# Windowed attention and a sticky mixture of experts on one core: the 128-partition attention transfers cut into 120 and 8 partitions

## The chip, the core and the metric

The kernel runs on one core of a Trainium2 chip, as one launch. The metric is the device time of the launch in microseconds (us). The core has five engines that run their own instruction streams: TensorE (PE in the profile, its weight loads PEld), VectorE (DVE), ScalarE (ACT), GpSimd (POOL) and SyncE (SP). Bulk data moves by DMA transfers, which an engine only issues; here SP issues all loads, ACT issues the stores of attention's result, and POOL issues the indirect gathers and scatters of the expert part.

## The reference

Two stages. The first is attention for 8 batches and 8 heads, with 32 global rows and 512 local rows of 64 numbers: a global row sees every row, a local row sees the global rows and the local rows at most 32 away. The second stage sends every token (a row of 8 x 64 = 512 numbers) through one of eight experts; a token keeps the expert of the token before it unless a local gate says otherwise.

```python
s_ll = np.where(np.abs(pos[:, None] - pos[None, :]) <= 32, s_ll, -1000000000.0)
out_l = softmax(concat([s_lg, s_ll])) @ concat([v_g, v_l])
...
fresh_e = argmax(x @ w_gate)
e = fresh_e if s == 0 or sigmoid(x @ w_local) < 0.5 else prev_e
out[b, s] = softmax(x @ w_gate)[e] * (relu(x @ w1[e]) @ w2[e])
```

## The kernel before

**Attention** runs from the start to about 275 us. Two heads make a pair, four pairs a batch, 32 pairs in all, numbered 0 to 31 here. A pair needs two loads of 128 partitions: its queries and keys (`load`, 128 x 1056 floats, 528 KB, array `qk`), and its values (`loadv`, 128 x 2080 floats, 1040 KB, array `vw`). A batch needs one more (`load_g`, 128 KB, its global queries). Query-and-key tiles stand in a ring of eight buffers (`hhl_a`, `wp_a`, `xhl_a`, `xr_a`, `raw` 0 to 3), value tiles in a ring of seven (`v` 0 to 3, `hhl_a`, `wp_a`, `v` 4; the names `hhl_a` and `wp_a` hold tiles of both kinds in different columns). `run` issues the loads ahead: queries and keys five pairs, values four pairs before the pair at which it stands. A load waits until the last reader of its buffer is done.

For each pair POOL copies the keys into `kx` (`prep`, L194), PE makes the scores (L240), DVE takes maximum and difference (L245, L247), ACT the exponential (L251), PE transposes (L257), ACT copies the result from PSUM into `pt` (L259), and PE multiplies with the values (L271). Work on the global rows (L291, L309, L323, L334) stands between pairs.

**The row stores.** When a batch is done and its keys and probabilities for the experts are made, `f4` writes its rows to the DRAM array `xs`, from which the experts gather. It issues six transfers on ACT: one of 128 partitions with four rows of 528 floats in each (1056 KB, L407), four of 32 partitions for the global rows (`xg`, 16 KB each, L411), and one of 2 KB (`gx`, L412). ACT runs its stream in order, so that the copies and exponentials behind these six wait until the last is issued. There are eight such stores, one for each batch; the first six fall among the pairs, the last two beside the first experts.

**Semaphores of transfers.** SP's and ACT's transfers share eight completion semaphores, DMAHW0 to DMAHW7, which are given out in turn when the program is built. A transfer first waits for the transfer that last held its semaphore, so at most eight are under way, and a store on ACT can wait for a load on SP, or the other way round. The turns go by the order in which the builder expects the transfers to be issued.

**Experts** fill the rest. Expert weights are loaded by SP into tiles of 512 KB (L1147), split by ACT and DVE into two parts (L1157, L1167), and used in PE's long runs of L1259 and L1270. The first three expert blocks overlap with the end of attention.

Of the kernel before, what the change touches and what calls it, by code (L numbers as in the profile page):

```python
# [18 lines left out]
P = 128  # L19
# [37 lines left out]
STORE = 2  # L57
AHEAD = 5
AHEADV = 4


def col(b):
    return 4 * b if b < NA else 4 * b + 1


def gcol(hf):
    return 4 * NA if hf == 0 else NT - 1
# [33 lines left out]
class Attn:  # L101
# [64 lines left out]
    def setup(self):  # L166
# [5 lines left out]
        yield  # L172
        nc.sync.dma_start(self.xs[0:P], zr)

    def load(self, b, pr):
        nc = self.nc
        if pr == 0:
            self.cur[b] = {"v": []}
        c = self.cur[b]
        t = c[("qk", pr)] = self.ld()  # L180
        nc.sync.dma_start(t, self.qk[b, pr])

    def load_g(self, b):
        g = self.cur[b]["qg"] = self.qgb()
        self.nc.sync.dma_start(g, self.qg[b])

    def loadv(self, b, pr):
        nc = self.nc
        v = self.v()
        self.cur[b]["v"].append(v)  # L190
        nc.sync.dma_start(v.rearrange("p w c -> p (w c)"), self.vw[b, pr])

    def cp(self, out, in_, pat):
        self.nc.gpsimd.affine_select(out=out, in_=in_, pattern=pat, compare_op=ALU.is_ge, fill=0.0, base=0, channel_multiplier=0)  # L194
# [205 lines left out]
    def f4(self, b, rt):  # L400
        nc = self.nc
        c = self.cur.pop(b)
        xa, xg = c["xa"], c["xg"]
        hf, b4 = b // 4, b % 4
        rq = slice(32 * b4, 32 * b4 + 32)
        r0 = P * (1 + col(b))
        nc.scalar.dma_start(self.xs[r0:r0 + 4 * P].rearrange("(t p) r -> p t r", p=P), xa)  # L407
        r0 = P * (1 + gcol(hf)) + 32 * b4
        xsg = self.xs[r0:r0 + 32]
        for h in range(4):  # L410
            nc.scalar.dma_start(xsg[:, 0:DM].rearrange("q (a h d) -> q a h d", a=2, h=4)[:, :, h], xg[32 * h:32 * h + 32])  # L411
        nc.scalar.dma_start(xsg[:, DM:ROW], rt.gx[rq])  # L412

    def run(self, rt, moe):
# [20 lines left out]
        for k in range(1, AHEAD):  # L435
            b, i = pairs[k]["u"]
            self.load(b, i)
            if i == 0 or k == 1:
                self.load_g(b)
            if k <= AHEADV:  # L440
                self.loadv(*pairs[k - 1]["u"])
# [11 lines left out]
        for s in range(n):  # L453
# [8 lines left out]
            if nl:  # L462
                if npr + AHEAD < len(pairs):
                    b, i = pairs[npr + AHEAD]["u"]
                    self.load(b, i)
                    if i == 0:
                        self.load_g(b)
                if npr + AHEADV < len(pairs):
                    self.loadv(*pairs[npr + AHEADV]["u"])
                npr += 1  # L470
# [1109 lines left out]
```

## Time and profile before

| what | value |
|---|---|
| median of three runs | 729.78 us (729.25, 729.78 and 739.17) |
| the profiled execution | 738.59 us, span 736.9 us |
| mean granted TensorE clock in it | 0.959 |
| PE busy | 661.8 us, 90% of the span |
| DVE, ACT, POOL busy | 422.4, 343.9 and 152.5 us |
| bytes by SP's queue (q1) | 117.72 MB |
| bytes by ACT's queue (q10) | 9.33 MB |
| attention's transfers of 128 partitions | 72 loads (32 + 32 + 8) and 8 row stores |

The profiled execution stands near the upper of the three runs, 8.8 us above their median. In the profile, "ACTq" and "SPq" are the issue of transfers on these engines: such a row's duration is the time in which the engine could do nothing else, not the time of the transfer, which is shown apart as the time to landing. Times in rows of the timeline and of the chain are counted from the start of the span.

### The profile page before, as it was taken

How to read it: one execution, taken by the hardware profiler on the slowest of the kernel's cores; microseconds unless marked ns; L12 is line 12 of the kernel's file. 1: busy time of each engine (PE TensorE's matmuls, PEld its weight loads, DVE VectorE, ACT ScalarE, POOL GpSimd, SP SyncE). 2: the span in 40 equal slices, each digit the busy share in tenths (PEclk: the TensorE clock that was granted, in tenths of full speed). 3: DMA queues.
4: the chain of work that ended last, by engine and by line, in shares of the span. 5: the costliest groups of instructions: out<-in, count | busy, mean ns of one | idle time of the engine just before them, and what ended most of it. 6: DMA issues, size and time to landing. Idle time of an engine off the chain costs nothing.

```text
span 736.9 us, 20404 instructions
## 1 busy us (share of the span) xinstructions
PE 661.8 (90%) x8277; PEld 551.8 (75%) x8277; DVE 422.4 (57%) x1052; ACT 343.9 (47%) x613; POOL 152.5 (21%) x259
## 2 busy tenths in 40 slices
PE   8689888687878869989899899999999999999996
PEld 6467656565656558779688788988888988988994
DVE  6566666655678666689732663533553634436563
ACT  4355545453545446464432753524353525345463
POOL 6112111121102130203121430304031202031122
PEclk9889989989989998999999999999999999999999
DMA  9976575847561455777662765725564725435763
GB/s 355 412 302 261 194 298 200 303 176 259 189 210 61 152 177 182 273 224 240 196 244 84 239 216 193 230 94 174 180 201 141 239 75 169 139 138 184 270 235 116
DMA packets 43019, 151.57 MB, mean 206 GB/s; under 512 B 7965, under 2 KB 9245, under 8 KB 38688
## 3 DMA queue, kind: packets, MB, share of 16 engines
q1 hardware_dynamic: 28368, 117.72, 45.5%
q0 software_dynamic: 6960, 21.90, 9.2%
q10 hardware_dynamic: 7456, 9.33, 3.7%
q8 instruction: 85, 1.39, 0.8%
q14 instruction: 150, 1.23, 0.5%
HBM read 130.55 MB, written 19.69 MB: 204 GB/s over the span
## 4 chain that ended last, share of the span: by engine, by line
PE 77%; DVE 10%; issue 5%; ACTq 3%; ACT 2%; DMA 1%; POOL 0%; DVEq 0%; POOLq 0%
PE ps L1270 27%; PE ps L1259 24%; PE ps L240 5%; PE ps L271 4%; PE ps L257 4%; PE ps L1212 3%; PE ps L347 2%; ACTq L411 2%; PE ps L291 2%; PE ps L334 2%; PE ps L323 2%; DMA xs<-xg 1%; DVE wp L1167 1%; DVE pe L247 1%; DVE mx L245 1%
## 5 line engine op out<-in xcount | busy, mean ns | idle before, releaser
L1270 PE MATMUL ps<-wp,wq 128*128 128x512 f32 x504 | 128.0, 401 | 1.0 <-ACT wq L1373 1.0
L1259 PE MATMUL ps<-wp,wp 128*128 128x256 f32 (+6 forms) x672 | 107.8, 320 | 1.5 <-issue 1.5
L1270 PEld LDWEIGHTS ps<-wp,wq 128*128 128x128 f32 x504 | 93.5, 190 | 20.8 <-ACT wq L1373 1.2
L1259 PEld LDWEIGHTS ps<-wp,wp 128*128 128x128 f32 x672 | 103.4, 189 | 5.5 <-issue 2.0
L1276 POOL DMA_INDIRECT out_dram<-y,tk x39 | 40.5, 1040 | 321.2 <-ACT y L1275 248.0
L1262 DVE SCALAR_TENSOR_TENSOR wq<-ps,wq 128x256 fp32r<-128x256 f32 (+6 forms) x80 | 41.3, 519 | 72.9 <-ACT wq L1261 65.2
L1261 ACT ACTIVATE wq<-ps 128x256 fp32r<-128x256 f32 (+6 forms) x80 | 36.8, 463 | 78.5 <-PE ps L1259 69.8
L1215 DVE TENSOR_TENSOR wp<-ps,wp 128x512 fp32r<-128x512 f32 x40 | 27.5, 691 | 79.7 <-ACT wp L1214 79.7
L245 DVE TENSOR_REDUCE mx<-ps 128x4 f32<-128x512 f32 x64 | 43.9, 685 | 36.4 <-PE ps L240 36.1
L1275 ACT ACTIVATE y<-ps,pp 128x512 f32<-128x512 f32 x39 | 26.9, 689 | 77.2 <-PE ps L1270 71.1
L251 ACT ACTIVATE pe<-pe 128x512 f32<-128x512 f32 x64 | 40.5, 633 | 40.8 <-DVE pe L247 40.3
L1167 DVE TENSOR_TENSOR wp<-raw,wp 128x1024 fp32r<-128x1024 f32 x47 | 56.9, 1217 | 2.8 <-ACT wp L1157 2.8
L1198 POOL DMA_INDIRECT xa<-xs,idx x42 | 51.3, 1221 | 17.1 <-issue 9.7
L259 ACT COPY pt<-ps 128x512 f32<-128x512 f32 x64 | 35.1, 595 | 40.3 <-DMA xs<-xg 17.7
L1157 ACT CAST wp<-raw 128x1024 fp32r<-128x1024 f32 x49 | 50.8, 1047 | 5.2 <-issue 3.8
L1214 ACT CAST wp<-ps 128x512 fp32r<-128x512 f32 x40 | 23.4, 590 | 55.2 <-PE ps L1212 55.2
L271 PE MATMUL ps<-v,pt 128*32 128x65 f32 x1536 | 31.4, 231 | 15.5 <-ACT pt L259 7.2
L247 DVE TENSOR_TENSOR pe<-ps,mx 128x512 f32<-128x512 f32 x64 | 44.1, 688 | 1.4
L1270 PE MATMUL ps<-hhl,wq 128*128 128x512 f32 x174 | 44.8, 398 | 0.0
L271 PEld LDWEIGHTS ps<-v,pt 128*32 128x32 f32 x1536 | 25.8, 115 | 25.1 <-ACT pt L259 10.4
L194 POOL TENSOR_SCALAR_AFFINE_SELECT kx<-raw 128x128 f32<-128x128 f32 (+1 forms) x64 | 21.9, 366 | 102.4 <-issue 76.9
L257 PE MATMUL ps<-idf,pe 128*128 128x128 f32 x256 | 39.9, 305 | 1.4 <-ACT pe L251 1.4
(284 smaller groups left out, 1168.5 us busy)
## 6 DMA issues: line engine op xcount, KB each, us to landing
raw<-in_w_dram SPq DMA_DIRECT2D x78, 512.0 KB, 4.1
v<-in_vw_dram SPq DMA_DIRECT2D x24, 1040.0 KB, 9.3
xa<-in_w_dram SPq DMA_DIRECT2D x26, 512.0 KB, 3.9
xT<-in_w_dram SPq DMA_DIRECT2D x20, 512.0 KB, 3.7
raw<-in_qk_dram SPq DMA_DIRECT2D x16, 528.0 KB, 6.5
xs<-xa ACTq DMA_DIRECT2D x8, 1056.0 KB, 7.4
hhl_a<-in_vw_dram SPq DMA_DIRECT2D x4, 1040.0 KB, 11.2
wp_a<-in_vw_dram SPq DMA_DIRECT2D x4, 1040.0 KB, 4.8
```

The lines of the kernel that those rows point to most:

```text
L245: nc.vector.tensor_reduce(out=mx, in_=st["sp"][h], axis=AX.X, op=ALU.max)
L247: nc.vector.tensor_tensor(out=st["pe"][:, 4 * h:4 * h + 4], in0=st["sp"][h], in1=mx.broadcast_to([P, 4, P]), op=ALU.subtract)
L251: self.nc.scalar.activation(out=pe, in_=pe, func=AF.Exp, scale=SCALE)
L257: nc.tensor.transpose(tp[:, i], st["pe"][:, 4 * hb + i], self.cst.idf)
L271: nc.tensor.matmul(o[32 * w4:32 * w4 + 32, t], pt[:, t, w4, :], v[:, 4 * t + w4, h * (D + 1):(h + 1) * (D + 1)], start=True, stop=True, sk ...
L1157: nc.scalar.copy(out=hi, in_=raw)
L1167: (nc.gpsimd if pool else nc.vector).tensor_tensor(out=lo, in0=raw, in1=hi.bitcast(F32), op=ALU.subtract)
L1198: self.nc.gpsimd.indirect_dma_start(out=self.xr[j] if k == "early" else self.xr4[:, j], out_offset=None, in_=src, in_offset=bass.IndirectO ...
L1259: nc.tensor.matmul(ph, a[:, dc, fs], b_[:, dc, n0:n1], start=(n == 0), stop=(n == 11))
L1262: nc.vector.scalar_tensor_tensor(out=hl[:, fc, n0:n1], in0=ph, scalar=0.0, in1=hh[:, fc, n0:n1].bitcast(F32), op0=ALU.max, op1=ALU.subtract)
L1270: nc.tensor.matmul(py, a[:, fc, js], b_[:, fs], start=(fc == 0 and k == 0), stop=(fc == 7 and k == 2))
L1276: sc = nc.gpsimd.indirect_dma_start(out=self.out, out_offset=bass.IndirectOffsetOnAxis(ap=self.g[1][:, j:j + 1], axis=0), in_=y, in_offset ...
```

## The change

Each of attention's loads of 128 partitions, and each row store, is made by two transfers, one of partitions 0 to 119 and one of partitions 120 to 127, on the same engine and one right after the other. The loads of weights, the small stores and the indirect transfers stay as they are, and so does all arithmetic.

```diff
+CUT = 120
...
+    def get(self, to, of):
+        for r in (slice(0, CUT), slice(CUT, P)):
+            self.nc.sync.dma_start(to[r], of[r])
...
-        nc.sync.dma_start(t, self.qk[b, pr])
+        self.get(t, self.qk[b, pr])
...
-        self.nc.sync.dma_start(g, self.qg[b])
+        self.get(g.rearrange("p a h q -> p (a h q)"), self.qg[b])
...
-        nc.sync.dma_start(v.rearrange("p w c -> p (w c)"), self.vw[b, pr])
+        self.get(v.rearrange("p w c -> p (w c)"), self.vw[b, pr])
...
-        nc.scalar.dma_start(self.xs[r0:r0 + 4 * P].rearrange("(t p) r -> p t r", p=P), xa)
+        x = self.xs[r0:r0 + 4 * P].rearrange("(t p) r -> p t r", p=P)
+        for r in (slice(0, CUT), slice(CUT, P)):
+            nc.scalar.dma_start(x[r], xa[r])
```

SP issues 72 transfers more and ACT eight more. They take turns at the same eight semaphores, so these turn over about twice as fast. Three places show it.

The first is ACT's stream at the row store of batch 0, before and after; the row behind the transfers is the copy into `pt` of the pair under way (`xa0` is the batch's rows, `xg0` its global rows, a number behind a name is that of the buffer).

```order
L407 DMA xs_57<-xa0_104 128x4x528 [waits DMAHW7_49]
L411 DMA xs_57<-xg0_107 32x2x64 [waits DMAHW0_49]
L411 DMA xs_57<-xg0_107 32x2x64 [waits DMAHW1_49]
L411 DMA xs_57<-xg0_107 32x2x64 [waits DMAHW2_49]
L411 DMA xs_57<-xg0_107 32x2x64 [waits DMAHW3_49]
L412 DMA xs_57<-gx_287 32x16 [waits DMAHW4_49]
L259 COPY pt2_140<-ps4_67 128x512 [waits PE_49,Activation_49]
```

```order
L412 DMA xs_57<-xa0_104 120x4x528 [waits DMAHW2_49]
L412 DMA xs_57<-xa0_104 8x4x528 [waits DMAHW4_49]
L416 DMA xs_57<-xg0_107 32x2x64 [waits DMAHW6_49]
L416 DMA xs_57<-xg0_107 32x2x64 [waits DMAHW0_49]
L416 DMA xs_57<-xg0_107 32x2x64 [waits DMAHW1_49]
L416 DMA xs_57<-xg0_107 32x2x64 [waits DMAHW2_49]
L417 DMA xs_57<-gx_300 32x16 [waits DMAHW4_49]
L262 COPY pt2_140<-ps4_67 128x512 [waits PE_49,Activation_49]
```

Before, the six transfers hold six different semaphores. After, the turns of SP's loads lie between them, and the last `xg` transfer waits for DMAHW2, which the 120-partition store took five rows above it, while the `gx` transfer waits for DMAHW4, which the 8-partition store took.

The second is SP's stream around the same store, before and after: the loads from the values of pair 10 (`v2`) to those of pair 12 (`hhl_a`).

```order
L191 DMA v2_132<-in_vw_dram 128x2080 [waits DMAHW2_49,PE_49]
L181 DMA xr_a_86<-in_qk_dram 128x1056 [waits DMAHW3_49,Pool_49]
L191 DMA v3_133<-in_vw_dram 128x2080 [waits DMAHW4_49,PE_49]
L181 DMA raw0_77<-in_qk_dram 128x1056 [waits DMAHW5_49,PE_49,Pool_49]
L185 DMA qgb1_149<-in_qg_dram 128x256 [waits DMAHW6_49,PE_49]
L191 DMA hhl_a_88<-in_vw_dram 128x2080 [waits DMAHW7_49,PE_49]
```

```order
L178 DMA v2_132<-in_vw_dram 8x2080 [waits DMAHW3_49]
L178 DMA xr_a_86<-in_qk_dram 120x1056 [waits DMAHW5_49,Pool_49]
L178 DMA xr_a_86<-in_qk_dram 8x1056 [waits DMAHW7_49]
L178 DMA v3_133<-in_vw_dram 120x2080 [waits DMAHW3_49,PE_49]
L178 DMA v3_133<-in_vw_dram 8x2080 [waits DMAHW5_49]
L178 DMA raw0_77<-in_qk_dram 120x1056 [waits DMAHW6_49,PE_49,Pool_49]
L178 DMA raw0_77<-in_qk_dram 8x1056 [waits DMAHW7_49]
L178 DMA qgb1_149<-in_qg_dram 120x256 [waits DMAHW0_49,PE_49]
L178 DMA qgb1_149<-in_qg_dram 8x256 [waits DMAHW1_49]
L178 DMA hhl_a_88<-in_vw_dram 120x2080 [waits DMAHW2_49,PE_49]
```

Before, the turns run on through these loads, and the store of batch 0 takes its turns only ten loads later, after the queries and keys of pair 16. After, it takes them here: the semaphores 2, 4, 6, 0, 1, 2 and 4 that are missing between the rows down to `v3`'s second are the store's. So the queries and keys of pair 12 (`raw0`) wait for the landing of the first `xg` transfer, and the values of pair 12 for that of the last. The next five stores stand the same way to the loads that begin with pairs 16, 20, 24, 27 and 31.

The third is SP's first loads, before from the queries and keys of pair 3 (`xr_a`) on, and after from the values of pair 0 (`v0`) on.

```order
L181 DMA xr_a_86<-in_qk_dram 128x1056
L191 DMA v2_132<-in_vw_dram 128x2080
L181 DMA raw0_77<-in_qk_dram 128x1056 [waits DMAHW0_49]
L185 DMA qgb1_149<-in_qg_dram 128x256 [waits DMAHW3_49]
L191 DMA v3_133<-in_vw_dram 128x2080 [waits DMAHW4_49]
```

```order
L178 DMA v0_130<-in_vw_dram 120x2080
L178 DMA v0_130<-in_vw_dram 8x2080
L178 DMA xhl_a_87<-in_qk_dram 120x1056 [waits DMAHW0_49]
L178 DMA xhl_a_87<-in_qk_dram 8x1056 [waits DMAHW1_49]
L178 DMA v1_131<-in_vw_dram 120x2080 [waits DMAHW3_49]
L178 DMA v1_131<-in_vw_dram 8x2080 [waits DMAHW5_49]
L178 DMA xr_a_86<-in_qk_dram 120x1056 [waits DMAHW6_49]
```

Before, the first eight loads wait for nothing and the ninth (`raw0`) for the landing of the first. After, the fifth load waits already, and each that follows waits for one about four loads ahead of it.

More of the change, by code (lines that the diff above doesn't have):

```diff
@@ L173, in setup @@
         nc.sync.dma_start(self.xs[0:P], zr)
+    def get(self, to, of):
+        for r in (slice(0, CUT), slice(CUT, P)):
+            self.nc.sync.dma_start(to[r], of[r])
     def load(self, b, pr):
-        nc = self.nc
         if pr == 0:
@@ L180, in load @@
         t = c[("qk", pr)] = self.ld()
-        nc.sync.dma_start(t, self.qk[b, pr])
+        self.get(t, self.qk[b, pr])
     def load_g(self, b):
         g = self.cur[b]["qg"] = self.qgb()
-        self.nc.sync.dma_start(g, self.qg[b])
+        self.get(g.rearrange("p a h q -> p (a h q)"), self.qg[b])
     def loadv(self, b, pr):
-        nc = self.nc
         v = self.v()
         self.cur[b]["v"].append(v)
-        nc.sync.dma_start(v.rearrange("p w c -> p (w c)"), self.vw[b, pr])
+        self.get(v.rearrange("p w c -> p (w c)"), self.vw[b, pr])
     def cp(self, out, in_, pat):
```

## The prediction, made before the changed kernel was timed

> **What bounds the kernel now.** I read the stretches first, then the chain of the first 275 us, then one row store in the timeline, then the issues of loads.
>
> The stretches (length, busy us of PE, PEld, DVE, ACT and POOL, TensorE clock, DMA share, GB/s):
>
> ```profile
> 0.00:37.00 37.00, 27.64 (x650) 20.77 (x650) 21.67 (x74) 14.52 (x31) 15.12 (x68) 0.92 0.97 384
> 37.00:275.00 238.00, 191.97 (x5017) 142.89 (x5015) 160.86 (x565) 116.70 (x261) 43.46 (x109) 0.92 0.59 213
> 275.00:737.00 462.00, 442.22 (x2612) 388.16 (x2612) 239.86 (x414) 212.63 (x321) 93.91 (x84) 0.98 0.57 188
> ```
>
> Three stages with different limits. To 37 us the DMA engines are busy 97% of the time, at 384 GB/s. To 275 us no unit is full: PE works 192 of 238 us and waits in short gaps. From there PE is busy 442 of 462 us. The change touches the first two, and of the third only its beginning.
>
> The chain of the first 275 us, by line, and six of its pieces (start, length, what):
>
> ```profile
> by line: PE ps L240 12.1%; issue 11.2%; PE ps L257 9.5%; PE ps L271 9.4%; PE ps L291 5.3%; PE ps L347 5.3%; PE ps L323 4.5%; ACTq L411 4.5%; PE ps L334 4.2%; DMA xs<-xg 3.7%; DVE pe L247 2.9%; DVE mx L245 2.8%; PE ps L233 2.4%; PE ps L362 1
> ...
> 31.27 3.54 issue
> ...
> 80.04 3.04 DMA xs<-xg
> ...
> 112.84 1.22 ACTq L411
> ...
> 164.35 3.65 issue
> ...
> 180.90 3.28 DMA xs<-xg
> ...
> 240.84 2.18 ACTq L411
> ```
>
> PE's own work leads. Two things beside it matter here. ACT's issue of the `xg` transfers has 4.5% and the piece that the profile names by the transfer, though ACT is only issuing there, 3.7%: 8.2% of 275 us, 22.6 us for seven row stores. And "issue", time in which PE waited for nothing that the profile shows, has 11.2%, 30.8 us.
>
> The row store of batch 0, ACT's issues and what stands behind them:
>
> ```profile
> 77.78 0.40 ACTq L407 DMA_DIRECT2D xs<-xa  x1
> ...
> 78.22 0.52 ACTq L411 DMA_DIRECT2D xs<-xg  x1
> ...
> 78.78 1.23 ACTq L411 DMA_DIRECT2D xs<-xg  x1
> ...
> 80.04 2.46 ACTq L411 DMA_DIRECT2D xs<-xg  x2
> ...
> 82.54 0.43 ACTq L412 DMA_DIRECT2D xs<-gx  x1
> 83.08 1.07 ACT L259 COPY pt<-ps 128x512 f32<-128x512 f32 x2 [3.93 <-DMA xs<-xg]
> 83.71 0.39 PEld L271 LDWEIGHTS ps<-v,pt 128*32 128x32 f32 x24 [2.66 <-ACT pt L259]
> 83.71 0.49 PE L271 MATMUL ps<-v,pt 128*32 128x65 f32 x20 [1.75 <-ACT pt L259]
> ```
>
> The six issues hold ACT for 5.19 us (77.78 to 82.97). The copy into `pt` comes right behind, and PE's L271 waits for that copy. So the end of the hold is on the path, and a longer hold is paid in full.
>
> How long transfers take: the times to landing of the row stores (L407) and of the loads of values (L191), and two medians from the table of issues.
>
> ```profile
> DMA to landing us min/median/max: 6.8/7.4/8.0
> ...
> DMA to landing us min/median/max: 4.8/9.3/12.5
> ...
> raw<-in_qk_dram SPq DMA_DIRECT2D x16, 528.0 KB, 6.5
> ...
> xs<-xg ACTq DMA_DIRECT2D x32, 16.0 KB, 6.9
> ```
>
> And the first and last issue of the largest of the six holds (batch 3, 6.13 us) and of the smallest (batch 4, 4.24 us):
>
> ```profile
> 177.95 0.38 ACTq L407 DMA_DIRECT2D xs<-xa  x1
> ...
> 182.73 1.35 ACTq L412 DMA_DIRECT2D xs<-gx  x1
> ...
> 204.09 0.41 ACTq L407 DMA_DIRECT2D xs<-xa  x1
> ...
> 207.87 0.46 ACTq L412 DMA_DIRECT2D xs<-gx  x1
> ```
>
> **The change, part by part.**
>
> *The hold of ACT at the first six row stores.* In the changed order the last `xg` transfer (at batch 5 the last but one) waits for the landing of the 120-partition store, which has just been issued. That store has fifteen sixteenths of a store that lands after 7.4 us; I take 7.4. Then ACT issues that `xg` transfer (0.52, the first of the rows above, with no queue ahead of it) and `gx` (0.43), whose wait for the 8-partition store I take as over by then: a hold of 8.35 us. The 8-partition store's own issue and the `xg` issues ahead lie inside the 7.4. Before, the six holds run from 4.24 to 6.13 us, in the mean 5.4. So 3.0 us more each, 18 us for six. Bounds: 6.8 + 0.52 + 0.43 against a hold of 6.13 gives 1.6 each, 10 us; 8.0 + 1.23 + 0.46 against 4.24 gives 5.4 each, 33 us. The mean over the six is nearest to what all six pay. All of it goes to the path, since L271 stands behind it.
>
> *The last two stores* wait for no transfer of their own. Each has one issue more, between 0.40 and 1.23 us: 0.8 each, 1.6 us.
>
> *The saturated start.* The bytes stay, in twice the transfers, and four loads are under way at most where there were eight:
>
> ```profile
> 4.58 0.47 SPq L181 DMA_DIRECT2D raw<-in_qk_dram  x1
> 8.83 0.33 SPq L185 DMA_DIRECT2D qgb<-in_qg_dram  x1
> ...
> 19.57 1.33 POOL L194 TENSOR_SCALAR_AFFINE_SELECT kx<-raw 128x128 f32<-128x128 f32 x4 [1.86 <-DMA raw<-in_qk_dram]
> ```
>
> The jump from 4.58 to 8.83 is SP waiting for a semaphore of the eight. Pair 4's load, issued at 4.58, lands at about 19.5, and POOL waits 1.86 us for it: the order of arrival limits here. If all is as fast as before, it costs nothing; if half of the engines carry nine rows where they carried eight, 37 us become 41.6. I take 4, near that end, since eight partitions don't spread evenly over sixteen engines, and both parts of a load must have landed.
>
> [...]
>
> *Loads behind the stores.* In the new order pair 12's loads wait for transfers of batch 0's store. The reading of pair 12 before:
>
> ```profile
> 45.19 0.33 SPq L181 DMA_DIRECT2D raw<-in_qk_dram  x1
> ...
> 80.45 0.29 POOL L194 TENSOR_SCALAR_AFFINE_SELECT kx<-raw 128x128 f32<-128x128 f32 x1 [6.62 <-issue]
> ...
> 94.30 1.16 PE L240 MATMUL ps<-kx,raw 64*32 64x128 f32 x64
> ...
> 103.08 0.98 PE L271 MATMUL ps<-hhl_a,pt 128*32 128x65 f32 x50
> ```
>
> Its queries and keys were loaded from 45.19, 33 us ahead of the store at 77.78. Counted from the store, its scores run at 16.5 us and its values are read at 25.3; with 3 us of longer hold at 19.5 and 28.3. After the change the first `xg` transfer is issued at about 1.7 (behind 0.40 and at most 1.23 for the two parts of the store), lands at 8.6 (6.9 after), and the load behind it lands at 15.9 with its two issues (0.4 each) and 6.5. POOL needs 1.3 for `kx`: 17.2, ahead of 19.5. The last `xg` transfer is issued at 7.4, lands at 14.3, and the values land at 24.4 (0.8 and 9.3), ahead of 28.3. Two and four microseconds of room, so nothing is paid; the cover is this room. With the slowest landing of values, 12.5, it is 27.6, still inside. I take 0, with bounds 0 and 2 us for each of six stores.
>
> *Issues on SP*: 72 more, 0.33 to 0.47 us each, some 30 us of an engine that mostly waits for buffers and runs ahead of the readers. Nothing waits for SP there beyond the terms above: 0. The weights' loads behind attention keep their form and take their turns as before: 0.
>
> *Sum*: 18 + 1.6 + 4 + 0 = 23.6 us. Made against the profiled execution it is 738.6 + 23.6 = 762.2. The median of the runs is 729.8, and the same microseconds on it give 753.4; I say 754. The third stage keeps its length, as PE is full there by its own work.
>
> **Rivals.**
>
> *R1, the cut transfers are slow themselves.* The room above ends when the store and the values each take a few us more. If all cut transfers take half as long again, the store lands after about 11, and six holds grow by 3.7 each, 22 us; the values land at 11.1 + 6.9 + 0.8 + 14 = 32.8 where they are read at 32, 5 us for six; the start's 37 us grow by 18, 14 more than above. Together 23.6 + 22 + 5 + 14 = 65, so 794. At a quarter the stores add 11 and the start 5: 770. For it: the second stretch moves 213 GB/s with 384 seen, so at half speed (192) attention would be bound by DMA. Against: the wide transfers keep 15 of 16 parts of their rows. [...]
>
> *R2, no slower: less congestion pays for the hold.* The 30.8 us of "issue" seem to stand where bulk loads are in flight, like the gap at 31.27:
>
> ```profile
> 28.38 0.33 SPq L191 DMA_DIRECT2D v<-in_vw_dram  x1
> 30.89 0.33 SPq L181 DMA_DIRECT2D xhl_a<-in_qk_dram  x1
> ```
>
> If these gaps come from sharing the DMA engines, four loads in flight instead of eight could take most of them: with 24 us gone the sum is 0, 730; it decides from 9 us up, where the total falls within 2% (744.4). Against: that gap, one of the longest, came with these two loads just issued, fewer than the four that stay allowed, and after the change loads come in bursts behind each store.
>
> *R3, the wait is there but its cost is hidden*: the new wait coincides with gaps that PE has anyway. Then only about half of the hold is paid: 729.8 + 9 + 5.6 = 744. Against it are the rows of L259 and L271 above.
>
> **Chances.** The forecast 0.50, with a range of its own from 741 to 768 (18 us going from 10 to 33, the start from 0 to 5); R1 0.25; R2 0.12; R3 0.13. The range reaches from R2's better half to R1's middle: 738 to 796. A measurement of this kernel can tell about 2% from no change, 15 us. Slower by over 2%: 0.45 of the forecast (its low end lies within 2%), R1's 0.25 and 0.05 of R3, 0.75. Within 2%: 0.22. Faster: 0.03.
>
> **What will show it.** Hold: ACT's six row stores last 8 to 9 us, with a gap ahead of the last `xg` issue that ends with the landing of L412's first transfer, while the last two stay near 5. Loads: pair 12's keys are issued after the first store, not 33 us ahead, and POOL's L194 hardly waits for DMA. R1: landing of the 120-partition loads well above 9.3, the DMA share of 37 to 275 us far over 0.59. R2: "issue" in the chain under 7%. Wrong altogether: holds of 5 us (the store's semaphore is no wait), or POOL's L194 waiting for transfers at each store, which is a lost lead and not a hold.

## The result, and the profile after

| | before | after |
|---|---|---|
| median of three runs | 729.78 us | 819.25 us (809.17 to 822.03) |
| the profiled execution, its span | 738.59, 736.9 us | 819.25, 817.5 us |
| mean granted TensorE clock in it | 0.959 | 0.906 |

The ratio is 1.111, with a 95% interval from 1.085 to 1.137: 81 us more (62 to 100). It leaves out the run of 822.03 us, which counts as a slow one, and so is not the quotient of the two medians. The prediction said 754 us and a range of 738 to 796. It had the direction right and the size far too small.

The lines of the code that the profile names have moved by 3 to 5: L178 is now the issue of every cut load (in `get`), L197 POOL's copies into `kx`, L243 the scores, L274 the values' matmul, L262 the copy into `pt`, L412 the row store, L416 `xg`, L417 `gx`.

First the same stretches as before the change (length, busy us of PE, PEld, DVE, ACT, POOL, TensorE clock, DMA share, GB/s), of the changed kernel:

```profile
0.00:37.00 37.00, 24.28 (x474) 17.98 (x475) 16.75 (x53) 12.72 (x27) 12.95 (x62) 0.86 0.93 195
37.00:275.00 238.00, 169.93 (x3971) 127.17 (x3971) 121.27 (x423) 88.12 (x197) 29.60 (x88) 0.80 0.78 183
348.00:817.00 469.00, 443.89 (x2613) 391.04 (x2612) 240.26 (x418) 213.93 (x322) 95.96 (x84) 0.97 0.57 186
```

To 37 us the DMA engines are as busy as before (0.93 for 0.97) and move half: 195 GB/s for 384. Divide the two: 210 GB/s per full share, where it was 396. To 275 us it is 235 (183 at 0.78) for 361 (213 at 0.59). The bytes are the same, as SP's queue shows, but its packets take 52.3% of the engines' longer span instead of 45.5% of the shorter one:

```profile
q1 hardware_dynamic: 28872, 117.73, 52.3%
```

The last row of the stretches begins at the seventh row store, which moved from 272.34 to 348.36 us. From there to the end 469 us are left, where 464 were. So attention lost 76 us and the experts 5.

The chain of work through attention (0 to 370 us) of the changed kernel, by line, and its longest pieces:

```profile
by line: issue 16.1%; PE ps L274 8.9%; DMA v<-in_vw_dram 8.0%; PE ps L243 7.5%; DMA xs<-xa 7.0%; PE ps L260 6.2%; PE ps L294 4.5%; PE ps L350 4.3%; PE ps L326 4.2%; PE ps L337 3.8%; DMA xs<-xg 2.8%; PE ps L1264 2.5%; ACTq L416 2.0%; DMA qgb
...
2.75 6.74 DMA qgb<-in_qg_dram
9.51 14.73 DMA v<-in_vw_dram
...
64.47 4.66 issue
...
100.68 6.17 DMA xs<-xa
...
162.31 5.16 issue
...
202.97 14.77 DMA v<-in_vw_dram
228.91 6.73 DMA xs<-xa
```

Three kinds of pieces have grown beside PE's own lines. Loads that come late: the values have 8.0% of 370 us, 30 us, in two pieces, one at the start (9.51) and one at 202.97. ACT's hold at the row stores, which the profile names by the store (`xs<-xa`): 7.0%, 26 us. And "issue", PE waiting for nothing that the profile shows: 16.1%, 60 us, where it was 30.8 of 275. Added up piece by piece to the seventh row store, PE's own work has 164 us of the chain in both kernels. Of the 76 us more, "issue" has 29, the late values 30, ACT's row stores 19 and a late `qgb` 7, while DVE has 8 less; the rest is small.

PE's work itself became slower too. All of the work ahead of the seventh row store, before and after:

```profile
0.00:272.34 272.34, 219.61 (x5665) 163.67 (x5665) 182.39 (x637) 130.79 (x292) 56.42 (x175) 0.92 0.64 236
```

```profile
0.00:348.36 348.36, 248.56 (x5665) 185.52 (x5665) 183.38 (x637) 131.51 (x292) 56.03 (x175) 0.82 0.79 184
```

The same 5665 matmuls are busy for 248.56 us instead of 219.61, at a granted clock of 0.82 for 0.92, while DVE, ACT and POOL stay within 1 us. No run sets the clock by itself. So whether PE's longer waits pull it down, and how much of these 29 us the kernel pays, stays open.

The first row store of the changed kernel on ACT:

```profile
100.04 0.60 ACTq L412 DMA_DIRECT2D xs<-xa  x1
...
103.10 3.44 ACTq L416 DMA_DIRECT2D xs<-xg  x3
106.87 0.32 ACTq L417 DMA_DIRECT2D xs<-gx  x1
107.29 1.07 ACT L262 COPY pt<-ps 128x512 f32<-128x512 f32 x2 [5.46 <-DMA xs<-xg]
```

It holds ACT for 7.15 us (100.04 to 107.19), 5.19 before. SP issues the next loads right behind it, from 107.11 on, and POOL copies the keys of the first of them (pair 12):

```profile
107.11 0.67 SPq L178 DMA_DIRECT2D raw<-in_qk_dram  x2
...
109.43 0.67 SPq L178 DMA_DIRECT2D raw<-in_qk_dram  x2
...
112.23 1.33 POOL L197 TENSOR_SCALAR_AFFINE_SELECT kx<-raw 128x128 f32<-128x128 f32 x4 [21.11 <-DMA raw<-in_qk_dram]
```

And who waits for loads (who, us, times), from the view of the load's line L178:

```profile
  POOL kx L197: 198.6, 23
```

Against the prediction's "POOL's L194 hardly waits for DMA", POOL waits 198.6 us in 23 waits, where it waited 4.8 us in 4 before. The lead is lost. Not all of this is paid, since POOL's copies come ahead of PE's need: the scores of pair 12 run at 125.36, well behind the copy at 112.23.

### The profile page after: what moved, and what is told of

Read it like the earlier page. It is cut to its first block, busy times and chain, and to the rows that moved or that the text cites. A ratio compares the mean times of both kernels' runs of the same rounds, so it can differ in the third digit from the quotient of the medians.

```text
span 817.5 us, 20554 instructions
## 1 busy us (share of the span) xinstructions
PE 692.3 (85%) x8277; PEld 576.6 (71%) x8277; DVE 423.3 (52%) x1052; ACT 345.1 (42%) x613; POOL 152.0 (19%) x259
## 3 DMA queue, kind: packets, MB, share of 16 engines
q1 hardware_dynamic: 28872, 117.73, 52.3%
## 4 chain that ended last, share of the span: by engine, by line
PE 71%; DMA 9%; issue 8%; DVE 7%; ACT 2%; ACTq 2%; POOL 0%; SPq 0%; DVEq 0%; POOLq 0%
PE ps L1275 24%; PE ps L1264 22%; PE ps L274 4%; DMA v<-in_vw_dram 4%; PE ps L243 3%; DMA xs<-xa 3%; PE ps L260 3%; PE ps L1217 2%; PE ps L294 2%; PE ps L350 2%; PE ps L326 2%; PE ps L337 2%; DMA xs<-xg 2%; ACTq L416 1%; DMA qgb<-in_qg_dram 1%
## 5 line engine op out<-in xcount | busy, mean ns | idle before, releaser
L274 PE MATMUL ps<-v,pt 128*32 128x65 f32 x1536 | 38.8, 264 | 34.7 <-ACT pt L262 14.8
L274 PEld LDWEIGHTS ps<-v,pt 128*32 128x32 f32 x1536 | 32.2, 137 | 49.9 <-issue 24.6
L262 ACT COPY pt<-ps 128x512 f32<-128x512 f32 x64 | 35.2, 595 | 64.7 <-DMA xs<-xg 39.3
L197 POOL TENSOR_SCALAR_AFFINE_SELECT kx<-raw 128x128 f32<-128x128 f32 (+1 forms) x64 | 21.6, 367 | 138.9 <-DMA raw<-in_qk_dram 81.0
L260 PE MATMUL ps<-idf,pe 128*128 128x128 f32 x256 | 43.0, 323 | 0.0
```

Of the source, the lines that this page charges most:

```text
L260: nc.tensor.transpose(tp[:, i], st["pe"][:, 4 * hb + i], self.cst.idf)
L274: nc.tensor.matmul(o[32 * w4:32 * w4 + 32, t], pt[:, t, w4, :], v[:, 4 * t + w4, h * (D + 1):(h + 1) * (D + 1)], start=True, stop=True, sk ...
```

## The experiments

Five theories of why the loads are slow or late were set against each other; the expectations name them:

- T1: a cut transfer moves at about half the rate, because of where its rows lie. With it the author expected 64 + 64 (195 to 230 GB/s to 37 us) and rows 0 to 63 alone (200 to 280 per full share) to be slow, and 112 + 16 and rows 32 to 95 alone to be back at 340 to 390. How the rows of a transfer are dealt out to the DMA engines no run here shows.
- T2: the engines are only loaded unevenly (nine rows on some, eight on others); 112 + 16 and 64 + 64 would be at the full rate again.
- T3: the rate does not matter, but twice the transfers take the eight semaphores in turn.
- T4: the parts of 8 partitions are what is slow.
- T5: any transfer of fewer than 128 rows is slow, wherever the rows lie.

Ratios are against the kernel before, run on the same chip, with 95% intervals; microseconds are worked out from the ratio and the median of before in that session (732 to 735 us).

### Loads alone, stores alone

From the changed kernel, one of the two edits is undone.

```diff
 # a_loads_cut: the row store whole
-        for r in (slice(0, CUT), slice(CUT, P)):
-            nc.scalar.dma_start(x[r], xa[r])
+        nc.scalar.dma_start(x, xa)
 # b_stores_cut: the loads whole
-        for r in (slice(0, CUT), slice(CUT, P)):
-            self.nc.sync.dma_start(to[r], of[r])
+        self.nc.sync.dma_start(to, of)
```

> Only the loads are made as 120 + 8, the row stores are whole as before. [...] T2 (the engines are only loaded unevenly, nine rows on some for eight): the start is some 4 us longer and the time is 733 to 745. [...] This run tells T2 from the others.

> Only the row stores are made as 120 + 8, the loads are whole as before. T1: the loads keep 384 GB/s in the first 37 us; the row stores are about 9 MB beside 118 MB of loads, so that little is lost beside longer holds of ACT: 735 to 755. T2: the same, 733 to 750. T3: the semaphores turn by one more for each store only: 730 to 750. If the time is over 790, the stores carry the loss and all three fall.

Loads alone: 806.23 us, ratio 1.092 (1.078 to 1.106), 67 us. Stores alone: 748.28 us, 1.024 (1.014 to 1.035), 18 us. Together 85, and both at once cost 81: the two add up. The stretch to 37 us, with the loads cut:

```profile
0.00:37.00 37.00, 24.33 (x474) 17.71 (x475) 16.86 (x53) 12.62 (x27) 12.94 (x62) 0.82 0.92 197
```

and with the stores cut:

```profile
0.00:37.00 37.00, 28.41 (x695) 21.29 (x698) 22.51 (x76) 15.29 (x33) 15.71 (x70) 0.91 0.97 384
```

The loads carry the slow rate. T2 is out with them: it gave 733 to 745.

### Other places of the cut

`c_cut_112` and `d_cut_64` change one number of the changed kernel, so that number and order of the transfers stay. In the traces their issues name the same semaphores in the same order as in the changed kernel:

```diff
-CUT = 120
+CUT = 112    # d_cut_64: 64
```

> [...] T3: nothing that counts has changed against 120 + 8: 805 to 825.

> [...] T3: 805 to 825 with a DMA share well under 0.9. [...]

112 + 16: 794.2 us, 1.082 (1.073 to 1.090). 64 + 64: 817.53 us, 1.116 (1.107 to 1.125). Their stretches to 37 us, first of 112 + 16:

```profile
0.00:37.00 37.00, 24.43 (x575) 18.07 (x576) 18.27 (x60) 12.91 (x28) 14.22 (x66) 0.94 0.98 243
```

then of 64 + 64:

```profile
0.00:37.00 37.00, 28.05 (x601) 20.74 (x601) 19.14 (x66) 13.79 (x30) 13.08 (x62) 0.91 0.97 211
```

Two equal halves are as slow as 120 + 8: 211 GB/s at 0.97, 218 per full share. Both parts have 64 rows for the 16 DMA engines, so T2 has nothing uneven to point to, and no part is small: T2 and T4 fall. That 112 + 16 would be back at 340 GB/s was wrong: it has 243 (248 per full share), a little better and still slow. So T1 had one hit and one miss, and T5 was open. T3 as the only cause falls here: it gave both kernels 805 to 825, and with the same turns 112 + 16 is 23 us faster than 64 + 64.

### The same number of transfers, cut by columns

```diff
 # e_columns; the row store likewise, at 15/16 of its 528 columns
-        for r in (slice(0, CUT), slice(CUT, P)):
-            self.nc.sync.dma_start(to[r], of[r])
+        n = of.shape[-1] * 15 // 16
+        for c in (slice(0, n), slice(n, None)):
+            self.nc.sync.dma_start(to[:, c], of[:, c])
```

> Loads and stores are cut in two as in the changed kernel, at the same places of the program and with the same shares of bytes (15/16 and 1/16), but by columns: either part keeps all 128 partitions. The number of transfers, their order and the turns of the eight semaphores are those of the changed kernel. [...] T3 (twice the transfers and four loads in flight cost the time): 795 to 825. [...]

747.55 us, 1.021 (1.015 to 1.028), 16 us. The rate to 37 us of this kernel:

```profile
0.00:37.00 37.00, 26.94 (x697) 20.71 (x698) 22.31 (x76) 15.44 (x33) 15.83 (x70) 0.93 0.95 351
```

Each part keeps all 128 partitions, and 351 GB/s at 0.95 are 369 per full share. The whole loss, 16 us, is no more than what the cut stores cost alone (18). So near the full rate twice the transfers, on semaphores that turn over twice as fast, cost nothing that can be measured beside the stores.

But the turns are not those of the changed kernel, though the expectation took them to be. The builder gave the semaphores out otherwise, and the loads keep most of their lead. When a row store began, so many loads of queries and keys, and of values, had been issued:

| kernel | batch 0 | batch 1 | batch 2 | batch 3 |
|---|---|---|---|---|
| before | 17 and 15 | 21 and 19 | 25 and 23 | 29 and 27 |
| changed | 12 and 11 | 16 and 15 | 20 and 19 | 24 and 23 |
| cut by columns | 16 and 14 | 21 and 19 | 25 and 23 | 29 and 27 |

From batch 1 on SP runs as far ahead as before the change. What the lost lead would cost at the full rate is therefore not shown by this run, nor by any other.

### Rows 0 to 63 against rows 32 to 95

The first use of each buffer loads all rows; later loads bring one block of rows in one transfer, so that there are as many transfers as before the change. The other rows keep the data of an earlier load, which changes what is computed for them.

```diff
 # f_rows_120_alone: rows 0 to 119; i_rows_0_64: 0 to 63; j_rows_32_96: 32 to 95
+        k = of.shape[-1]
+        first = self.used.get(k, 0) < (2 if k == 256 else 8)
+        self.used[k] = self.used.get(k, 0) + 1
+        r = slice(0, P) if first else slice(32, 96)
+        self.nc.sync.dma_start(to[r], of[r])
```

> Stores whole. The loads are whole for the first use of each buffer and then of partitions 0 to 119 alone: the other eight rows keep the data of an earlier load (the output is another, and the routing may be too). There are as many transfers and turns as before the change, and no small part. T1: from 100 to 275 us the DMA engines move what they moved per busy share in the changed kernel (183 GB/s at 0.78 is 235 per full share; 200 to 260 here), and POOL waits for loads. T4 (the parts of 8 partitions are what is slow, or the number of transfers): 340 to 380 per full share, as before the change (213 at 0.59 is 361).

> Stores whole. After the first use of each buffer the loads bring partitions 0 to 63 alone, in one transfer (the other rows keep data of an earlier load; the output is another, and so may the routing be). [...] T5 (any transfer of 64 rows goes at one rate): the same figure as in the next kernel.

> [...] T2, T5 and any cause in the size, the number or the unevenness of transfers: both kernels alike within 3% in GB/s per full share and in time.

A single run of each gave 775.71, 740.05 and 718.1 us. The same three kernels, in four runs each:

> The kernel that loads partitions 0 to 119 alone after the first use of each buffer, timed in rounds (one look had 775.7). The rate by itself: 770 to 782.

> Partitions 0 to 63 alone after the first use of each buffer, timed in rounds (one look had 740.1). T1: 15 us or more above the next kernel. T5: within 1% of it.

> Partitions 32 to 95 alone after the first use of each buffer, timed in rounds (one look had 718.1). T1: 713 to 724, below the kernel before. T5: no difference from rows 0 to 63.

Rows 0 to 119: 771.68 us, 1.052 (1.043 to 1.061). Rows 0 to 63: 741.1 us, 1.013 (1.006 to 1.020). Rows 32 to 95: 714.54 us, 0.975 (0.968 to 0.982). From 100 to 275 us, rows 0 to 63 first:

```profile
100.00:275.00 175.00, 141.07 (x3794) 106.83 (x3793) 123.81 (x435) 87.04 (x195) 32.72 (x82) 0.94 0.54 133
```

then rows 32 to 95:

```profile
100.00:275.00 175.00, 139.33 (x3578) 107.35 (x3578) 121.46 (x420) 88.07 (x194) 30.75 (x70) 0.94 0.41 132
```

and before the change:

```profile
100.00:275.00 175.00, 137.86 (x3532) 102.01 (x3530) 118.17 (x411) 82.65 (x185) 31.87 (x74) 0.91 0.55 193
```

The same 64 rows' worth of bytes, in transfers of one size, goes at 246 GB/s per full share (133 at 0.54) from rows 0 to 63 and at 322 (132 at 0.41) from rows 32 to 95; the kernel before has 351. Whole row stores, and from 236 us on at the earliest loads of weights, are among all three. The time differs by 27 us in the medians and by 21.6 in the profiled executions (spans 737.9 and 716.3). Of these 21.6, attention has the larger part: the seventh row store starts 15.5 us later with rows 0 to 63 (first row below) than with rows 32 to 95 (second fence). The other 6 lie behind it, where the routing, which is another in either kernel, may have a part.

```profile
274.31 0.38 ACTq L415 DMA_DIRECT2D xs<-xa  x1
```

```profile
258.81 0.38 ACTq L415 DMA_DIRECT2D xs<-xa  x1
```

In the loads only the place of the rows differs. T5 is out: the place sets the rate. The 322 is a little under the 340 that was expected.

What in the place does it was not shown; the runs have the two rates of this pair, 246 against 322. That 64 + 64, one part of which is rows 0 to 63, is slow (218 to 37 us) agrees with the pair. Why 112 + 16 lies between (248) was not tested apart.

### What the rate does without the turns

With whole first loads, rows 0 to 119 alone cost 38 us (31 to 45), in the old turns (its issues in attention name the semaphores of the kernel before in the same order). Its stretch from 100 to 275 us, and the chain there:

```profile
100.00:275.00 175.00, 130.97 (x3258) 97.35 (x3256) 104.33 (x378) 74.12 (x167) 25.95 (x73) 0.86 0.71 173
```

```profile
by line: issue 20.2%; PE ps L247 12.6%; PE ps L264 10.2%; PE ps L278 8.0%; PE ps L354 6.0%; PE ps L341 5.8%; PE ps L298 5.3%; PE ps L330 4.8%; DVE mx L252 2.6%; PE ps L240 2.6%; PE ps L387 2.0%; ACTq L419 2.0%; DVE pe L254 1.9%; DVE o L912 
```

The rate is slow without any small part, 244 GB/s per full share (173 at 0.71), so T4 falls here too. No load stands among the pieces, so none is late, though T1 had POOL waiting for loads; "issue" has 20.2% of 175 us, 35 us. Where PE stands then can be seen in its own rows (the single run of rows 0 to 119):

```profile
150.60 0.84 PE L247 MATMUL ps<-kx,hhl_a 64*32 64x128 f32 x35
155.80 1.10 PE L247 MATMUL ps<-kx,hhl_a 64*32 64x128 f32 x29 [4.36 <-issue]
```

PE stops for 4.36 us in the middle of 64 matmuls of one kind, all of whose data are there. So I counted PE's records (weight loads, matmuls and its sequencer's, in order of start) ahead of each such pause. Most of the pauses over 1.5 us come after records number 705, 1217, 1473, 1985, 2753 and so on, all of them 193 more than a multiple of 256: 9 of 13 before the change, 12 of 17 after it, 14 of 16 with rows 0 to 119. Among the records from 300 to 9000 (to 213 us of the kernel before) there are 34 such places. The sum of PE's pauses at these 34 alone:

| kernel | pauses at the 34 places, us |
|---|---|
| before | 24.5 |
| changed | 53.9 |
| rows 0 to 119 alone | 53.6 |
| rows 0 to 63 alone | 33.2 |
| rows 32 to 95 alone | 15.9 |
| cut by columns | 22.2 |

They grow with the slow rate, by 29 us for rows 0 to 119, and they shrink when half the bytes come at a good rate. Up to the seventh row store that kernel is 33 us longer than the one before (305.36 for 272.34), and its matmuls are busy 10.8 us longer (230.40 for 219.61, at a clock of 0.88 for 0.92). So the pauses are the larger part; what the clock adds was not set apart.

The profile has two queues of the kind "instruction" beside the bulk, and counts their packets in the time of the same 16 DMA engines. One of them carries packets of 16 KB, 86 in the changed kernel:

```profile
q8 instruction: 86, 1.41, 0.8%
```

The trace holds the time of each packet. For the pause of 5.16 us at 162.31 in the changed kernel, the queues from the pause's start to 164.80, then from 164.80 to 166.15:

```profile
q1 hardware_dynamic: 67, 0.49, 91.2%
q14 instruction: 1, 0.01, 1.3%
```

```profile
q1 hardware_dynamic: 59, 0.25, 87.5%
q8 instruction: 1, 0.02, 6.2%
```

The bulk (q1) has over 87% of the DMA engines all the while. The packet comes 2.5 us after PE has stopped, and PE goes on 1.3 us after its end. So it is with every pause over 1.5 us at the 34 places: 9 of 9 before the change, 12 of 12 after it and 14 of 14 with rows 0 to 119 have one packet of q8 in flight, and PE goes on 1.2 to 1.7 us after its end. Over the 34 places there are 33, 34 and 33 such packets. Of the other pauses over 1.5 us, 6 of 11 have such a packet, with no fixed distance to its end.

So in all 35 of these pauses PE goes on shortly after a packet of q8 has ended. That PE waits for what the packet brings is the author's inference from these times and from the queue's kind; that the packet comes late because bulk stands ahead of it fits the growth under the slow rate, from 24.5 us before to 53.9 after. No run sets either apart.

### The parts of the loads' loss

`k_start_cut` cuts only the loads of the start, `m_late_loads_cut` only those behind the first use of each buffer; stores whole in both. Loads 7 and 8 of the values are whole in both.

```diff
 # k_start_cut (m_late_loads_cut: cut where n > 2 for k == 256, n > 8 for the others)
+        k = of.shape[-1]
+        n = self.used[k] = self.used.get(k, 0) + 1
+        for r in ((slice(0, CUT), slice(CUT, P)) if n <= {1056: 8, 2080: 6}.get(k, 2) else (slice(0, P),)):
+            self.nc.sync.dma_start(to[r], of[r])
```

> Only the loads of the start are made as 120 + 8 (eight of queries and keys, six of values, two of qg; those issued in the first 23 us before the change); all later loads and the stores are whole. This is the prediction's term of 4 us alone. T1 (half the rate): 12 to 25 us, 745 to 757. T2 (nine rows for eight): 4 us, 732 to 740.

> The first use of each buffer is loaded whole, all later loads are made as 120 + 8; stores whole. By difference of the earlier runs (806 with all loads cut, 753 with those of the start cut, 733 before) it should be at 780 to 792. Against the next kernel, which has the same slow transfers without the second parts and their turns: if the rate by itself makes the loss, the two are within 10 us; if the turns at the slow rate do, this one is 15 us or more above it.

The start: 753.07 us, 1.026 (1.018 to 1.033), 19 us. The later loads: 789.54 us, 1.077 (1.069 to 1.085), 57 us (51 to 62). Of these 57 the rate by itself makes 38 (rows 0 to 119 alone). The other 19 come with the second parts: their turns, and a sixteenth more of the bytes. The start and the later loads make 76 us together, where all loads cut cost 67 (57 to 78). How they come shows in the chain from 100 to 275 us of `m_late_loads_cut`:

```profile
by line: issue 18.1%; DMA v<-in_vw_dram 13.4%; PE ps L246 9.1%; DMA xr_a<-in_qk_dram 6.1%; PE ps L263 5.5%; PE ps L277 5.2%; PE ps L329 4.0%; DMA raw<-in_qk_dram 3.5%; DMA xs<-xa 3.5%; PE ps L340 3.5%; DVE mx L251 2.6%; PE ps L353 2.6%; DVE
```

Now loads are late: values, `xr_a` and `raw` have 23.0% of the stretch. Fewer loads stand ahead of the stores in this kernel (17 of queries and keys and 15 of values at batch 1, for 21 and 19 before). Slow transfers, four in flight and loads that wait for a store cost something together that the rate with the old turns (rows 0 to 119) does not. How the 19 us divide among them was not tried.

### Small parts on POOL's queue

```diff
 # l_tail_on_pool; row stores whole
+        self.nc.sync.dma_start(to[0:CUT], of[0:CUT])
+        self.nc.gpsimd.dma_start(to[CUT:P], of[CUT:P])
```

> Stores whole; the parts of 120 partitions are issued on SP as in the changed kernel, the parts of 8 partitions on POOL's queue, so that SP's transfers are as many as before the change and take the semaphores in the old turns. It tells what the slow rate costs without the turns. If the rate alone does it: 785 to 810 (the run with loads cut and whole stores had 806). If the turns, at half the rate, carry a large part, with loads held back behind stores: 755 to 785.

816.47 us, 1.111 (1.104 to 1.118), above both ranges. This was meant to take the turns away and could not tell: its first 37 us have a new wait of their own. POOL must now issue eleven small parts, and wait for some of them, before it makes what PE needs first (issues from 1.39 to 13.55 us, 6.3 us of waits for loads among them):

```profile
0.00:37.00 37.00, 9.46 (x164) 7.21 (x164) 8.88 (x23) 2.54 (x3) 20.98 (x76) 0.89 0.92 185
```

PE works 9.46 us there instead of 24.28.

### The row stores on another queue

From the kernel before, all six transfers of a row store are issued on SP, or on POOL:

```diff
 # g_stores_sp, in f4, three places (h_stores_pool: nc.gpsimd)
-        nc.scalar.dma_start(
+        nc.sync.dma_start(
```

> The kernel before, with all six transfers of each row store issued from SP's queue instead of ACT's. If the hold of ACT is what its chain says (8.2% of the first 275 us, 22.6 us) and SP has the time, 705 to 722. If the loads then stand behind the stores on SP as they did after the change, they still come at the full rate: pair 12's load would be issued some 5 us after the store instead of 33 us ahead, and that is worth 0 to 3 us a store, 710 to 745. Slower than 745 would show that the lead itself is what matters.

> The kernel before, with all six transfers of each row store issued from POOL's queue instead of ACT's. POOL is busy 43 of 238 us in attention, so a hold of some 5 to 10 us there should be covered by its lead: 705 to 725. If making the descriptors takes POOL longer, or kx comes late because of it, 730 to 760.

On SP: 722.4 us, 0.987 (0.981 to 0.992). On POOL: 729.25 us, 0.995 (0.992 to 0.998), between its two ranges; the issue of the 1056 KB takes POOL 0.79 us, where it took ACT 0.38. SP's first row store:

```profile
71.78 0.38 SPq L407 DMA_DIRECT2D xs<-xa  x1
72.21 3.76 SPq L411 DMA_DIRECT2D xs<-xg  x4
76.07 0.38 SPq L412 DMA_DIRECT2D xs<-gx  x1
76.55 0.38 SPq L181 DMA_DIRECT2D raw<-in_qk_dram  x1
```

Loads stand behind the store here too, at the full rate, and the kernel is still 10 us faster than the one before. But its lead shrinks by two pairs at the most (15 and 14 loads at the first store, for 17 and 15), so it does not settle what the larger loss of lead would cost. Taking the hold from ACT gave under half of the 22.6 us that its pieces have in the chain. It is the best of the kernels that compute everything.

## Why the prediction was wrong

**The step that failed is the rate.** Every duration of a cut transfer was taken from a whole one: the 120-partition store "has fifteen sixteenths of a store that lands after 7.4 us; I take 7.4", and pair 12's values land after the 9.3 of whole loads. The share of the bytes was kept, but the rate fell to half (210 GB/s per full share for 396). The start and the loads behind it rest on these durations. A second step failed with it: the sum left "issue" at its 30.8 us, though slow transfers lengthen it.

- *The hold at the stores*, 18 us and 1.6 for the last two, together 19.6: the size came out, the reason did not, and that is luck. Cutting the stores alone costs 18 us (10 to 26). But in that kernel the seven transfers of each store hold seven different semaphores (the trace has them with each issue), so none waits for its own store, and the first six holds still last 7.0 us in the mean, where they were 5.4. In the changed kernel the first six last from 7.15 to 9.84 us (306.42 to 316.26, the sixth), 7.8 in the mean, where 8.35 was forecast. The last two wait for no transfer of their own and last 7.3 and 7.1, where 5 was forecast. So the holds are about as long without the wait for the own store as with it. That the chain names the store behind ACT's hold (from 100.68 to 106.85 at the first) proves no such wait: it also does so in the kernel with the stores alone cut (6.85 us at 239.01). Why the issues behind a cut store take longer was not tried.
- *The saturated start*, 4 us: too small. It is 19 (13 to 24). The priced reason, nine rows on an engine that had eight, no run shows. What the runs show in its place is the rate: 195 GB/s to 37 us for 384, and no more than 211 with two parts of 64 rows.
- *Loads behind the stores*, 0 us with bounds to 12: this is the term that sinks the sum. The loads behind the start cost 57 us (51 to 62). The order of issues came as read (SP issues pair 12's keys at 107.11, behind the store). But the room held for these keys: POOL has copied these keys 13.5 us after the store's start (112.23 and 1.33), where 17.2 was forecast. On the chain of the changed kernel a single load behind the start is late, the values at 202.97 (14.8 us), while "issue" grew by 29 us up to the seventh store. So most of the loss came by a way on which the term has no price. Whether 0 holds for the lost lead at the full rate is not shown.
- *SP's issues*, 0: right, by the run cut by columns, which has as many.
- *The third stage keeps its length*: 469 us for 464, nearly right.
- *The forecast's own range*: its upper end, with 33 us, 1.6 and 5 on 729.8, comes to 769 rather than 768, which changes nothing.

**R1**, the slow transfers, is what happened, but beyond its price. It held that half the speed, 192 GB/s, would bind attention, and then worked out the sum for half as long again, 794. The argument against it, that wide transfers keep 15 of 16 parts of their rows, says nothing of where the rows lie. Even so its working at twice as long would have missed one thing: it priced slow loads only where they land too late. Rows 0 to 119 alone cost 38 us without a late load from 100 to 275 us.

**R2**, shorter pauses with less congestion, had the link right and the sign wrong. The "issue" pauses do depend on what the DMA engines carry (15.9 us at the 34 places with half the bytes at a good rate, 24.5 before); the changed kernel has the engines busy for longer with the same bytes (0.79 of 348.36 us to the seventh row store, for 0.64 of 272.34), and there they have 53.9. **R3** falls with the total: its 744 lies far below 819. That the cut stores cost only half of the hold cannot be told from their 18 us (10 to 26).

The signs that the prediction listed told it: the DMA share of 37 to 275 us went from 0.59 to 0.78, "issue" to 16.1% instead of under 7%, and POOL waits for transfers, which it had named as the case in which it is wrong altogether. Its sign that the last two holds stay near 5 us failed as well.

## What to carry to other kernels

Before a transfer is cut by partitions, ask where the rows of each part lie, not how many there are: here 128 rows in one transfer, or cut by columns, move 369 to 396 GB/s per full share of the DMA engines in the first 37 us, 120 + 8 and 64 + 64 about 215. From 100 to 275 us, where whole loads have 351, 64 rows go at 246 from rows 0 to 63 and at 322 from rows 32 to 95. A transfer that is hidden can have a price even so: with rows 0 to 119 alone no load was late from 100 to 275 us, and PE's pauses at the 34 places grew from 24.5 to 53.6 us. A duration read from a whole transfer is no bound for a cut one: price the rival that halves the rate to its end. And before a run is taken to hold the turns of the semaphores fixed, compare them in its trace.

## What the runs showed of the hardware

- The rate of a transfer into SBUF depends on which partitions it covers: 246 GB/s per full share for rows 0 to 63, 322 for rows 32 to 95, with the same number and size of transfers (whole stores and some loads of weights are among both).
- PE's long pauses come for the most part (9 of 13 before, 12 of 17 after) at places 256 records apart, 24.5 us in all before the change, and grow to 54 us under slow bulk transfers, whether or not a load is late. A packet of 16 KB on an instruction queue lies in each of them over 1.5 us (35 of 35 in three kernels), and PE goes on 1.2 to 1.7 us after its end.
- The granted clock to the seventh row store was 0.92 before and 0.82 after the change, and the same matmuls took 248.56 us for 219.61. What sets it was not tried.
- A row store issued on SP in place of ACT gives 1.3% (0.8 to 1.9), though SP's loads then stand behind it.
